# Attention with a soft mixture of experts: 64-row halves on TensorE, norms applied per row after a turn back, no detour through DRAM, and a new order

## The chip, the cores and the metric

The kernel runs on one core of one Trainium2 chip. The metric is device time in microseconds (us) of one execution. The kernel before took 525.68, 535.65 and 528.47 us in three runs, the median is 528.47 us. The core's engines are TensorE (PE; its weight loads are shown apart as PEld), VectorE (DVE), ScalarE (ACT), GpSimd (POOL) and SyncE (SP), whose queue issues nearly all transfers.

## The reference, cut to what matters

```python
# q, k, v: (8, 8, 576, 64); M_prev: (8, 8, 64, 64); z_prev: (8, 8, 64)
scores = np.where(causal, -1e9, q @ k.T / 8)
a = exp(scores - rowmax); a /= a.sum(-1) + 1e-9
local = a @ v
q_p = where(q > 0, q, exp(q) - 1) + 1
mem_out = (q_p @ M_prev) / (q_p @ z_prev + 1e-6)
attn = g * mem_out + (1 - g) * local          # g = sigmoid(beta), one per head
x = attn as (4608, 512)                       # row = batch and position, column = head and d
logits = x @ phi                              # 32 slots: 8 experts with 4 slots each
slot_input = softmax_over_rows(logits).T @ x
slot_out[e] = relu(slot_input[e] @ w1[e]) @ w2[e]     # 8 experts, 512 -> 1024 -> 512
out = softmax_over_slots(logits) @ slot_out
```

## The kernel before, in words

All data are fp32. The attention runs over 32 pairs n (8 batches with 4 pairs of heads; a pair's two heads lie on the row halves 0 to 63 and 64 to 127). For each pair the scores of 576 queries are cut into row blocks: three blocks of 128 queries for each head (q1, q2, q3, with 256, 384 and 512 keys) and blocks a, b, z in which 64 queries of both heads lie below each other. The q blocks are computed as three fp32r products of high and low parts with 64 contracted rows (`op_s`, L433), the two heads side by side in the array; a, b and z are fp32 products on all 128 rows (L427), with a q that was laid out block-diagonally in DRAM. DVE adds the mask and takes the row maximum (`op_max`, L462), ACT takes exponentials and row sums (`op_exp`, L470). TensorE then turns the probabilities in blocks of 128 by 128 (`op_t`, L560), ACT or DVE copy the turned blocks to SBUF (`op_te`), and `op_av` (L598) multiplies by v with an output whose rows are head and d and whose columns are queries. The output so has queries along its free axis, and the softmax sums and memory norms, which were found per row, have to be spread along the columns: they are turned (`op_rt`, L481), written to DRAM (`op_rrw`, `op_nrw`) and read back broadcast over 64 partitions (`op_rrr` into `rm`, L497; `op_nrr` into `rb`, L546). The factor `rb` is multiplied into phi(q) (`op_qn`, L550), the memory product adds to the output (`op_mema`, L592 and L593), and `op_mo`, `op_xe` (L626 to L637) multiply by `rm`, add, and leave the result in `xt`, which has d along partitions.

Every 512 rows of x form a group (9 groups) for the mixture: logits (`op_x1`, L646), running softmax, a turn of x (`op_x3`, L712), weighted sums of rows (`op_x4`, L725). The last group is done in the `y` steps after the last pair. Then come the experts (`f1`, `f1t`, `f2`) and the combination with its output transfers (`comb`).

The order is written out by hand as a list, `SEQ`: every step is emitted in that order, and `pin` makes each engine keep it; the digit behind a colon names the PSUM slot. `EV` says which engine makes a copy. PSUM has two score tiles of two banks (psS), three one-bank tiles (psT) and one output bank (psO). Expert weights are 64 tiles of 512 KB; `WORD` says where the first 44 of them go: 28 have a place of their own and can be loaded early, 16 go into tiles that the attention has freed. The other 20 are loaded in the expert stage, into places whose weights were used, and the output is staged in such places too.

Of the kernel before, what the change touches and what calls it, by code (L numbers as in the profile page):

```python
# [23 lines left out]
GROUPS = [
    [("q3h0", 0, 512), ("q3h1", 512, 512)],
    [("q2h0", 0, 384), ("b", 384, 128), ("q2h1", 512, 384), ("a", 896, 64)],  # L30
    [("q1h0", 0, 256), ("z", 256, 576), ("q1h1", 768, 256)],
]
# [11 lines left out]
}  # L44

SEQ = """
gate@0 loadq@1 loadm@0 loadk@1 loadm@1 loadv@0 qhi@0 qmin@0 kn@0 s.zb@0:0 qlo@0 qexp@0 s.b@0 s.a@0 kl@0 qmin@1 qphi@0
s.q3@0:1 max.b@0 max.a@0 exp.b@0 norm@0:0 max.q3h1@0 s.q2@0 neps@0 max.q3h0@0 exp.q3h1@0 nmk@0 max.q2h1@0 s.q1@0:1
exp.q3h0@0 max.zb@0 max.q2h0@0 s.z@0 kn@1 exp.q2h1@0 nred@0 kl@1 exp.q2h0@0 qhi@1 s.a@1:0 nrw@0 s.b@1 max.q1h0@0
s.zb@1 exp.a@0 loadq@2 t.1@0:1 max.a@1 qexp@1 max.zb@1 qlo@1 max.q1h1@0 t.2@0:2 max.z@0 exp.q1h0@0 nrr@0 t.0@0:0  # L50
te.2@0 max.b@1 s.q2@1 qphi@1 exp.z@0 s.q3@1:1 loadk@2 max.q2h1@1 exp.q1h1@0 max.q2h0@1 te.0@0 norm@1:2 rec@0 s.q1@1:0
neps@1 te.1@0 exp.b@1 nmk@1 rt@0:0 t.4@0:2 rte@0 qhi@2 max.q3h1@1 t.3@0:1 rrw@0 te.4@0 t.5@0:0 max.q3h0@1 exp.q2h1@1
s.z@1 te.3@0 exp.a@1 te.5@0 qn@0 s.a@2:1 s.zb@2 exp.q3h1@1 av.0@0 nred@1 rrr@0 max.z@1 av.2@0 kn@2 exp.z@1 loadk@3
av.1@0 loadq@3 max.a@2 kl@2 exp.q2h0@1 av.6@0 nrw@1 av.3@0 max.q1h0@1 exp.q3h0@1 memb@0:2 max.q1h1@1 s.b@2 loadv@1
mema@0:1 exp.q1h0@1 t.2@1:0 mo@0 qmin@2 loadm@2 s.z@2:0 nrr@1 te.2@1 xe.1@0 exp.q1h1@1 t.5@1:0 xe.0@0 qlo@2 t.1@1:1
rec@1 te.5@1 t.0@1:2 max.zb@2 max.b@2 qexp@2 rt@1:0 s.q2@2 rte@1 exp.a@2 qphi@2 rrw@1 te.1@1 s.q1@2 max.q2h1@2 te.0@1
t.4@1:0 max.q2h0@2 t.3@1:1 te.4@1 norm@2:2 te.3@1 neps@2 s.q3@2:1 rrr@1 exp.q2h0@2 nmk@2 max.q1h1@2 qhi@3 memb@1:0
kn@3 av.0@1 max.q1h0@2 loadq@4 qlo@3 exp.b@2 qn@1 exp.q1h0@2 av.3@1 max.z@2 av.6@1 exp.q2h1@2 kl@3 av.1@1 max.q3h0@2
exp.q1h1@2 av.2@1 nred@2 exp.q3h0@2 x3.0@0:1 nrw@2 exp.z@2 mema@1:2 mo@1 loadv@2 max.q3h1@2 loadk@4 s.q2@3:0 xe.1@1
nrr@2 exp.q3h1@2 s.q3@3:1 xe.0@1 x3e.0@0 rec@2 qmin@3 loadm@3 s.b@3 max.q3h1@3 t.4@2:2 qexp@3 max.q3h0@3 t.5@2:0  # L60
# [1030 lines left out]
```

## Time and profile before

| | |
|---|---|
| three runs | 525.68, 535.65, 528.47 us |
| span of the profiled execution | 529.8 us (no other time is given for it) |
| PE / PEld busy | 461.3 us / 307.6 us |
| DVE, ACT, POOL busy | 378.0, 331.8, 124.5 us |
| moved by DMA | 101.78 MB, mean 192 GB/s |

A busy time is the share in which at least one instruction of the engine was under way, with the time in which its result drains; the chain of work that ended last gives 34% to PE, 24% to DMA and 24% to DVE. On PE, two instructions stand in the trace for one fp32 product, and one for a turn or an fp32r product.

### The profile page before, as it was taken

To read this page: it belongs to the slowest core of one execution; us is meant where nothing else is said; L and a number is where in the kernel's file an instruction comes from. 1 tells how busy PE (TensorE), PEld (TensorE's weight loads), DVE (VectorE), ACT (ScalarE), POOL (GpSimd) and SP (SyncE) were. 2 spreads that over 40 slices of the span, in tenths; PEclk is the share of its full clock that TensorE was granted. 3 is DMA by queue.
4 is the path that set the end of the run, shared out by engine and by line. 5 is a ranking of instruction groups with operands and counts; after the bars stand their busy time and mean duration, and the time that the engine had idled before them with its cause. 6 is when DMAs were issued, how large, how long until landed. Compare 5 with 4: busy or idle time off the path is not lost.

```text
span 529.8 us, 12019 instructions
## 1 busy us (share of the span) xinstructions
PE 461.3 (87%) x4042; PEld 307.6 (58%) x4042; DVE 378.0 (71%) x1314; ACT 331.8 (63%) x969; POOL 124.5 (23%) x138
## 2 busy tenths in 40 slices
PE   8989899789998899999897987889988869799983
PEld 5656566556656566665665664656655546444541
DVE  7879788776788589789767877478887747334232
ACT  5777677666777577766786676566874837312232
POOL 4223122332213214235221332223314200000000
PEclk9999999989999999999999999799999979999997
DMA  6544654765466445554654674275564666899989
GB/s 200 181 142 133 186 178 132 217 203 162 137 172 181 138 128 171 140 155 134 196 153 145 187 202 123 58 176 152 157 188 142 214 191 178 304 415 410 382 297 323
DMA packets 66285, 101.78 MB, mean 192 GB/s; under 512 B 11248, under 2 KB 41520, under 8 KB 66224
## 3 DMA queue, kind: packets, MB, share of 16 engines
q1 hardware_dynamic: 65936, 100.93, 60.7%
q8 instruction: 32, 0.52, 0.4%
q14 instruction: 29, 0.24, 0.2%
q10 hardware_dynamic: 288, 0.09, 0.1%
HBM read 91.25 MB, written 9.73 MB: 191 GB/s over the span
## 4 chain that ended last, share of the span: by engine, by line
PE 34%; DMA 24%; DVE 24%; SPq 6%; ACT 4%; issue 4%; POOL 1%; DVEq 0%; POOLq 0%; ACTq 0%
DMA rm<-rs 9%; PE psT L560 6%; DVE q L462 5%; PE psS L427 5%; PE oa L598 4%; PE psS L433 4%; DVE zq L462 3%; DMA q<-in_M_dram 3%; DMA rs<-rts 3%; DMA k<-in_k_dram 3%; PE pf L947 3%; PE pf L930 2%; DVE at L358 2%; PE psT L592 2%; PE pp L990 2%
## 5 line engine op out<-in xcount | busy, mean ns | idle before, releaser
L355 ACT COPY at<-psT 128x256 f32<-128x256 f32 (+1 forms) x202 | 86.4, 479 | 53.5 <-PE psT L560 50.5
L470 ACT ACTIVATE q<-q,nm 128x512 f32<-128x512 f32 (+2 forms) x160 | 97.6, 613 | 17.2 <-DVE nm L462 17.0
L598 PE MATMUL oa<-at,mv 128*64 128x320 f32 (+4 forms) x640 | 94.0, 430 | 3.6 <-DVE at L358 1.4
L427 PE MATMUL psS<-k,qq 128*128 128x256 f32 (+2 forms) x320 | 67.7, 324 | 15.3 <-DVE nm L462 12.6
L462 DVE CUSTOM_DVE_ANT_0 q<-psS,mv 128x512 f32<-128x512 f32 (+1 forms) x128 | 76.1, 612 | 4.4 <-PE psS L433 2.5
L433 PE MATMUL psS<-K,X 64*128 64x512 f32 (+2 forms) x576 | 70.9, 367 | 8.6 <-DVE nm L462 6.8
L560 PE MATMUL psT<-cs,q 128*128 128x128 f32 x480 | 75.2, 280 | 3.3 <-DVE xt L633 1.4
L470 ACT ACTIVATE zq<-zq,nm 128x256 f32<-128x256 f32 (+2 forms) x128 | 67.7, 532 | 9.7 <-DVE nm L462 9.2
L427 PEld LDWEIGHTS psS<-k,qq 128*128 128x128 f32 x320 | 50.8, 195 | 27.2 <-DVE nm L462 18.2
L560 PEld LDWEIGHTS psT<-cs,q 128*128 128x128 f32 x480 | 57.3, 146 | 9.5 <-issue 3.2
L433 PEld LDWEIGHTS psS<-K,X 64*128 64x128 f32 x576 | 46.4, 189 | 27.0 <-issue 10.0
L598 PEld LDWEIGHTS oa<-at,mv 128*64 128x64 f32 x640 | 38.3, 138 | 39.0 <-issue 24.9
L560 PE MATMUL psT<-cs,zq 128*128 128x128 f32 x288 | 48.5, 283 | 2.8 <-DVE xt L633 1.0
L505 POOL TENSOR_SCALAR qp<-qq 128x576 f32<-128x576 f32 x19 | 31.4, 1650 | 68.2 <-PE psT L593 53.8
L626 DVE TENSOR_TENSOR xt<-oa,rm 128x448 f32<-128x448 f32 (+7 forms) x60 | 23.8, 436 | 30.3 <-DMA rm<-rs 25.4
L358 DVE COPY at<-psT 128x512 f32<-128x512 f32 (+1 forms) x59 | 32.4, 570 | 11.0 <-PE psT L560 9.7
L411 POOL TENSOR_TENSOR K<-k,K 128x512 fp32r<-128x512 f32 x25 | 32.4, 1295 | 33.3 <-ACT K L355 19.6
L550 DVE TENSOR_TENSOR qp<-qp,rb 128x576 f32<-128x576 f32 x32 | 27.6, 863 | 15.5 <-DMA rb<-rd 15.5
L560 PEld LDWEIGHTS psT<-cs,zq 128*128 128x128 f32 x288 | 34.9, 147 | 6.4 <-ACT at L355 1.7
L592 PE MATMUL psT<-qp,q 128*128 128x512 f32 x64 | 34.6, 622 | 2.9 <-DVE qp L550 1.9
L530 POOL TENSOR_TENSOR rn<-rn,rm 128x144 f32<-128x144 f32 x22 | 10.3, 467 | 100.2 <-ACT rn L523 57.4
L470 ACT ACTIVATION_READ_ACCUMULATOR q<-q,nm 128x1 f32 x160 | 31.1, 194 | 0.0
(207 smaller groups left out, 737.1 us busy)
## 6 DMA issues: line engine op xcount, KB each, us to landing
w<-in_w_dram SPq DMA_DIRECT2D x49, 512.0 KB
qq<-in_q_dram SPq DMA_DIRECT2D x32, 480.0 KB
mv<-in_v_dram SPq DMA_DIRECT2D x64, 160.0 KB
k<-in_k_dram SPq DMA_DIRECT2D x32, 288.0 KB
rb<-rd SPq DMA_DIRECT2D x64, 144.0 KB
rm<-rs SPq DMA_DIRECT2D x64, 144.0 KB
q<-in_M_dram SPq DMA_DIRECT2D x32, 80.0 KB
out_dram<-w SPq DMA_DIRECT2D x5, 512.0 KB
```

What stands on the lines that cost most here:

```text
L355: nc.scalar.copy(o, i)
L358: nc.vector.tensor_copy(out=o, in_=i)
L411: ALU_ENG[ev("kl", n)].tensor_tensor(out=K2[:, 1, :], in0=st[n]["k"][:, 0:512], in1=K2[:, 0, :].bitcast(F32), op=ALU.subtract)
L427: nc.tensor.matmul(ps[:, c + x0 - k0:c + x1 - k0], s["qd"][:, i], s["k"][:, x0:x1], start=True, stop=True)
L433: nc.tensor.matmul(ps[:, c0:c0 + N], X[ROW[h], x, 128 * i - 128:128 * i], K2[ROW[h], y, 0:N], start=(x, y) == (0, 0), stop=(x, y) == (0, 1))
L462: nc.vector.tensor_tensor_reduce(out=sm, in0=src, in1=msk, op0=ALU.add, op1=ALU.min, scale=-0.125, scalar=m0, accum_out=acc_o)
L470: nc.scalar.activation(sm, sm, AF.Exp, scale=-1.0, bias=s["nm"][:, J:J + 1], accum_out=s["sum"][:, J:J + 1])
L505: ALU_ENG[ev("qmin", n)].tensor_scalar(out=st[n]["qp"], in0=st[n]["q"], scalar1=0.0, scalar2=None, op0=ALU.min)
L550: ALU_ENG[ev("qn", n)].tensor_tensor(out=s["qp"], in0=s["qp"], in1=s["rb"], op=ALU.mult)
L560: nc.tensor.transpose(out=ps[:, 128 * x:128 * x + 128], in_=src[:, k0:k0 + 128], identity=ident)
L592: nc.tensor.matmul(om, s["m"][:, 0:128], s["qp"][:, 64:576], start=True, stop=True)
L598: nc.tensor.matmul(o[ROW[h], col:col + nx], vt[:, c, ROW[h]], at[:, a0 + hs * h:a0 + hs * h + nx], start=start, stop=stop)
```

## The change

The list of heads, pairs and groups stays, nearly every step of the attention is written anew.

- **Row halves.** For each pair and head, queries 64 to 575 form four blocks i of 128 with 192, 320, 448 and 576 keys. All are fp32r products of high and low parts on row halves (`s_part`); the fp32 products a, b, z are gone. The second head's keys are stored in reverse, so that its masked ends meet the first head's. Queries 0 to 63 of two pairs are handled together in 16 small side steps (`op_as` to `op_aad`).
- **Half turns.** A block of 128 by 128 is turned by two products, one for rows 0 to 63 and one for rows 64 to 127 (`turn`, with 64 columns of the identity moving), into two banks.
- **Product with v.** It works on 32-column quarters (`quarters`, `op_av`).
- **Turn back.** The output is copied (`op_oe`) and turned back so that queries lie on partitions (`op_u`, turns and memory products in one tile). Sums and norms are then one number per row: `op_dn` and `op_mu` apply them on DVE, POOL adds the two parts (`op_ad`). All writes to and reads from DRAM for norms are gone, and with them `op_rrw`, `op_rrr`, `op_nrw`, `op_nrr`, `op_qn`, `op_mo` and `op_xe`.
- **PSUM.** Scores, turns and `op_u` share three tiles of two banks (psD); psO and psM have one bank.
- **Loads.** One transfer brings q and k of a pair (`qk`, 544 KB), one v and M (`vm`, 544.5 KB), both into two tiles; a third (`au`, 385 KB) serves two pairs. They come 32, 32 and 16 times.
- **Weights.** `WORD` has 36 entries (18 with a place of their own, 18 in freed tiles); 28 are loaded in the expert stage.
- **Order.** `SEQ` and `EV` are new; the mixture's group of queries 0 to 63 (`AG`) comes before groups 6 and 7, and group 7 is the last.

```diff
-    def op_rrw(n):
-        rts = st[n]["rts"]
-        rd = st[n]["rs"] = drm.tile([2, S], F32, name="rs")
...
-    def op_nrw(n):
-        rd = st[n]["rd"] = drm.tile([4, 2, 144], F32, name="rd")
-        nc.sync.dma_start(out=rd.rearrange("g h (u x) -> (g h u) x", x=9), in_=st[n]["rq"])
...
-    def op_mema(n):
...
+    def s_part(n, ps, i, c, k0, k1):
+        s = st[n]
+        for x, y in ((0, 0), (1, 0), (0, 1)):
+            for h in range(2):
+                o = h * (S - LEN[i])
+                nc.tensor.matmul(ps[:, h, c:c + k1 - k0], s["X"][ROW[h], x, 128 * i:128 * i + 128], s["K"][ROW[h], y, o + k0:o + k1],
+                                 start=(x, y) == (0, 0), stop=(x, y) == (0, 1))
...
+    def turn(o, i, r):
+        nc.tensor.transpose(out=o, in_=i, identity=ident[ROW[r], ROW[r]])
+
+    def op_t(n, t):
+        s = st[n]
+        ps = s["t", t] = bank()
+        full = {"A": [(3, kb, h) for kb in range(4) for h in range(2)],
+                "B": [(2, kb, h) for kb in range(3) for h in range(2)],
+                "C": [(1, kb, h) for kb in range(2) for h in range(2)] + [(0, 0, h) for h in range(2)]}[t]
+        for x, (i, kb, h) in enumerate(full):
+            for r in range(2):
+                turn(ps[:, r, 64 * x:64 * x + 64], s["p", i][ROW[r], h, (128 * kb, 64 + 128 * (i - kb))[h]:][:, 0:128], r)
+        for x, i in {"A": (), "B": ((6, 3), (7, 2)), "C": ((6, 1), (7, 0))}[t]:
+            turn(ps[:, 1, 64 * x:64 * x + 64], s["p", i][ROW[1]].rearrange("a h x -> a (h x)")[:, LEN[i] - 64:LEN[i] + 64], 1)
...
+    def quarters(o, w, rhs, start, stop):
+        for j in range(4):
+            nc.tensor.matmul(o[32 * j:32 * j + 32], w[:, 32 * j:32 * j + 32], rhs[j // 2], start=start, stop=stop)
...
+        for kb in range(i + 1):
+            quarters(o, s["v"][:, kb], [at[:, 2 * kb + h, i].rearrange("a r x -> a (r x)") for h in range(2)], kb == 0, False)
+        quarters(o[:, 64:128], s["vb"][:, i], [atq[:, 3 - i]] * 2, False, True)
...
+    def op_u(n, u):
+        s, u = st[n], int(u)
+        ps = s["u", u] = bank()
+        for x in range(2):
+            i = 2 * u + x
+            for h in range(2):
+                turn(ps[:, h, 130 + 65 * x:194 + 65 * x], s["os"][ROW[h], 128 * i:128 * i + 128], h)
+        for x in range(2):
+            i = 2 * u + x
+            for h in range(2):
+                nc.tensor.matmul(ps[:, h, 65 * x:65 * x + 65], s["f"][ROW[h], 128 * i:128 * i + 128], s["m"][ROW[h]], start=True, stop=True)
...
+        nc.vector.tensor_tensor(out=w, in0=s["u", u][:, :, 0:260].rearrange("a h (x d) -> a h x d", d=65)[:, :, :, 0:64],
+                                in1=s["R"][:, u].rearrange("a h (x o) -> a h x o", o=1).broadcast_to([128, 2, 4, 64]), op=ALU.mult)
...
+        ALU_ENG[ev(f"ad.{u}", n)].tensor_tensor(out=o, in0=w[:, :, 0:2], in1=w[:, :, 2:4], op=ALU.add)
```

How the order on PE changes is seen in the steady middle. In the kernel before, around pairs 10 and 11, the rows of PE are these (a row is a line, the tile written and read, the output's partitions by columns, and how many products; 32 partitions are quarters, 64 are column halves, L433 works on row halves):

```order
L433 MATMUL psS_2030<-K_104,X 128x256 x6
L725 MATMUL psT_2063<-xk,ext 32x256 x4
L518 MATMUL psT_2070<-qp,q_1995 32x144 x4
L598 MATMUL oa<-at,mv 64x512 x2
L598 MATMUL oa<-at,mv 64x64 x2
L598 MATMUL oa<-at,mv 64x320 x2
L598 MATMUL oa<-at,mv 64x192 x2
L598 MATMUL psT_2102<-at,mv 64x64 x2
L598 MATMUL oa<-at,mv 64x448 x2
L433 MATMUL psS_2110<-K_104,X 128x512 x6
L592 MATMUL psT_2126<-qp,q_1822 128x512
L593 MATMUL psT_2102<-qp,q_1822 128x64
```

In the changed kernel, at about the same place (L391 scores, L426 half turns, L488 and L543 products on row halves, L454 quarters):

```order
L426 MATMUL psD_3557<-cs,p_3459 128x64 x14
L391 MATMUL psD_3576<-K,X 128x288 x6
L391 MATMUL psD_3589<-K,X 128x448 x6
L543 MATMUL psD_3604<-au 128x64 x4
L426 MATMUL psD_3611<-cs,os 128x64 x4
L488 MATMUL psD_3611<-vm,f 128x65 x4
L454 MATMUL oa<-at,vm 32x128 x4
L454 MATMUL oa<-at,vm 32x64 x4
L454 MATMUL oa<-at,vm 32x128 x8
L454 MATMUL oa<-at,vm 32x64 x4
L426 MATMUL psD_3654<-cs,x 128x64 x8
L426 MATMUL psD_3666<-cs,p_3515 128x64 x16
```

Before, the array changes its tile shape after one to six rows (row halves, quarters, column halves, full); now all but the quarters work on row halves, and the shape changes at `op_av` alone. Over the whole program the shape changes 275 times before and 143 times now.

The queue of SP before, for about one pair (`rd`, `rs` are the tiles in DRAM, `rb` and `rm` what is read back):

```order
L540 DMA rd<-rq 128x9
L391 DMA mv<-in_v_dram 64x640 x2
L546 DMA rb<-rd 64x4x144 x2
L396 DMA q_1995<-in_M_dram 128x160
L491 DMA rs<-rts 3x128 x2
L492 DMA rs<-rts 2x2x64
L493 DMA rs<-rts 2x1x64
L381 DMA qq<-in_q_dram 128x960
L749 DMA w_2077<-in_w_dram 128x1024
L386 DMA k<-in_k_dram 128x576
L497 DMA rm<-rs 64x576 x2
```

And now, for about two:

```order
L347 DMA qk<-in_qk_dram 128x1088
L354 DMA vm<-in_vm_dram 128x1089
L739 DMA w_2941<-in_w_dram 128x1024
L347 DMA qk<-in_qk_dram 128x1088
L522 DMA au<-in_au_dram 128x770
L354 DMA vm<-in_vm_dram 128x1089
```

Nothing that an engine has just computed goes through this queue any more, and an input load stands behind no such transfer.

## Rows read from the trace of the kernel before

**Rows 1.** The page, busy time of each engine over the span.
```profile
PE 461.3 (87%) x4042; PEld 307.6 (58%) x4042; DVE 378.0 (71%) x1314; ACT 331.8 (63%) x969; POOL 124.5 (23%) x138
```

**Rows 2.** Stretches: attention, joint, experts (us; busy and count; clock; DMA share; GB/s).
```profile
7.50:455.70 448.20, 396.86 (x3330) 273.68 (x3330) 347.14 (x1236) 310.02 (x923) 122.34 (x130) 0.98 0.55 162
455.70:469.70 14.00, 10.49 (x154) 7.63 (x152) 8.44 (x31) 4.32 (x14) 0.00 (x0) 1.00 0.99 397
469.70:529.90 60.20, 47.91 (x552) 23.36 (x552) 18.62 (x37) 14.53 (x28) 0.00 (x0) 0.94 0.96 360
```

**Rows 3.** Chain of work that ended last, its longest pieces in the attention (start, us, what).
```profile
309.95 5.84 DMA rm<-rs
...
423.79 8.10 DMA q<-in_M_dram
```

**Rows 4.** Waits of PE in the attention (us in total, times, longest us).
```profile
PE psS L427 <- DVE nm L462: 12.6, 18, 2.1
PE psT L518 <- DMA q<-in_M_dram: 10.2, 3, 5.0
```

**Rows 5.** Timeline of PE (start us, us, engine, line): full weights, 32 moving columns.
```profile
467.77 1.06 PE L862 MATMUL psT<-lt,xk 128*128 128x32 f32 x8
468.66 0.36 PE L877 MATMUL psT<-den,cs 128*128 128x1 f32 x2
```

**Rows 6.** Timeline of PE: row halves, quarters, row halves.
```profile
7.50 0.97 PE L433 MATMUL psS<-K,X 64*128 64x512 f32 x6
8.40 0.45 PE L518 MATMUL psT<-qp,q 128*32 128x144 f32 x8
8.79 0.80 PE L433 MATMUL psS<-K,X 64*128 64x384 f32 x6
```

**Rows 7.** Stretches cut between pairs of row halves, 384 columns, then 512.
```profile
63.39:63.57 0.18, 0.18 (x4) 0.18 (x4) 0.00 (x0) 0.18 (x1) 0.00 (x0) 1.00 0.62 128
63.97:64.20 0.23, 0.23 (x4) 0.19 (x2) 0.00 (x0) 0.23 (x1) 0.00 (x0) 1.00 0.96 381
```

**Rows 8.** Timeline of PE: column halves of 64 columns, then row halves.
```profile
62.79 0.28 PE L598 MATMUL psT<-at,mv 128*64 128x64 f32 x4
62.90 0.29 PE L598 MATMUL oa<-at,mv 128*64 128x64 f32 x4
63.12 1.49 PE L433 MATMUL psS<-K,X 64*128 64x384 f32 x12
```

**Rows 9.** Timeline of PE: 32 quarter products of 128 columns, then full ones.
```profile
124.01 1.08 PE L646 MATMUL psT<-xt,rm 128*32 128x128 f32 x32
125.07 0.43 PE L427 MATMUL psS<-k,qq 128*128 128x64 f32 x2
```

**Rows 10.** Timeline of PE: four full turns, then the next instruction.
```profile
211.80 0.60 PE L560 MATMUL psT<-cs,zq 128*128 128x128 f32 x4
212.24 0.56 PE L427 MATMUL psS<-k,qq 128*128 128x64 f32 x4
```

**Rows 11.** Groups on DVE by line (count, busy us, mean ns, idle before, releaser).
```profile
L550 DVE TENSOR_TENSOR qp<-qp,rb 128x576 f32<-128x576 f32 x32 | 27.6, 863 | 15.5 <-DMA rb<-rd 15.5
L626 DVE TENSOR_TENSOR xt<-oa,rm 128x448 f32<-128x448 f32 (+7 forms) x60 | 23.8, 436 | 30.3 <-DMA rm<-rs 25.4 <-PE oa L598 3.2 <-PE psT L593 1.2
L637 DVE TENSOR_TENSOR xt<-xt,psT 128x448 f32<-128x448 f32 (+7 forms) x60 | 23.4, 429 | 0.8 <-PE psT L592 0.7
```

**Rows 12.** Timeline of DVE: row maxima of 256, then of 512 columns.
```profile
199.90 0.42 DVE L462 CUSTOM_DVE_ANT_0 zq<-psS,mv 128x256 f32<-128x256 f32 x1
200.24 0.75 DVE L462 CUSTOM_DVE_ANT_0 zq<-psS,mv,nm 128x512 f32<-128x512 f32 x1
```

**Rows 13.** Group on ACT: exponentials of 576 keys.
```profile
L470 ACT ACTIVATE zq<-zq,nm 128x576 f32<-128x576 f32 x32 | 24.7, 772 | 4.4 <-DVE nm L462 4.4
```

**Rows 14.** Two stretches: PE waiting in the attention; the experts' loads.
```profile
330.00:340.00 10.00, 7.01 (x45) 6.10 (x46) 2.33 (x12) 2.67 (x7) 2.51 (x3) 0.66 0.26 71
470.00:500.00 30.00, 29.02 (x338) 13.04 (x332) 7.57 (x20) 5.57 (x12) 0.00 (x0) 1.00 1.01 405
```

More of the change, by code (lines that the diff above doesn't have):

```diff
@@ L227 @@
[L227 to L231 removed]
+QK = 512 + S
@@ L354, in act, with misc @@
+    def misc():
+        return psM.tile([128, 512], F32, name="psM")
     def act(o, i):
@@ new lines, in op_as, with op_amx @@
+    def op_as(n):
+        s = us[n]
+        ps = s["ps"] = bank()
+        for x in range(2):
+            for h in range(2):
+                nc.tensor.matmul(ps[:, h, 0:64], s["q"][ROW[h], x], s["k"][ROW[h], x], start=x == 0, stop=x == 1)
+    def op_amx(n, h):
+        s, h = us[n], int(h)
+        if "nm" not in s:
+            s["nm"] = sml.tile([128, 2], F32, name="anm")
+            s["p"] = spl.tile([128, 2, 64], F32, name="ap")
+        nc.vector.tensor_tensor_reduce(out=s["p"][:, h], in0=s["ps"][:, h, 0:64], in1=mask2, op0=ALU.add, op1=ALU.min,
+                                       scale=-0.125, scalar=3.0e38, accum_out=s["nm"][:, h:h + 1])
@@ new lines, in op_aav, with op_aoe, op_au @@
+    def op_aav(n):
+        s = us[n]
+        s["oa"] = misc()
+        for x in range(2):
+            quarters(s["oa"][:, 64 * x:64 * x + 64], s["v"][:, x], [s["at"][:, x]] * 2, True, True)
+    def op_aoe(n):
+        s = us[n]
+        s["os"] = spl.tile([128, 128], F32, name="aos")
+        ENG[ev("aoe", n)](s["os"], s["oa"][:, 0:128])
+    def op_au(n):
+        s = us[n]
+        ps = s["u"] = bank()
+        for h in range(2):
+            turn(ps[:, h, 65:129], s["os"][ROW[h]], h)
+        for x in range(2):
+            for h in range(2):
+                nc.tensor.matmul(ps[:, h, 0:65], pha[ROW[h], x], s["m"][ROW[h], x], start=x == 0, stop=x == 1)
@@ new lines, in op_x3, with op_x3e @@
+    def op_x3(g, c):
+        d, c = xs[g], int(c)
+        ps = d["p3", c] = bank()
+        for j in range(4):
+            for r in range(2):
+                turn(ps[:, r, 64 * j:64 * j + 64], d["x"][ROW[r], j, 128 * c:128 * c + 128], r)
+    def op_x3e(g, c):
+        d, c = xs[g], int(c)
+        d["xd", c] = dbl.tile([128, 4, 2, 64], F32, name="xd", bufs=4)
+        ENG[ev(f"x3e.{c}", g)](d["xd", c].rearrange("a j r x -> a r j x"), d["p3", c][:, :, 0:256].rearrange("a r (j x) -> a r j x", j=4))
@@ new lines, in op_x1, with op_x1l @@
+    def op_x1(g, c=None):
+        if c is None:
+            for c in range(4):
+                op_x1(g, c)
+            return
+        d, c = xs[g], int(c)
+        if c == 0:
+            d["p1"] = misc()
+        for j in range(4):
+            nc.tensor.matmul(d["p1"][32 * j:32 * j + 32, 0:128], ph[:, c, :], d["xd", c][:, j].rearrange("a r x -> a (r x)"), start=c == 0, stop=c == 3)
+    def op_x1l(g):
+        lt = xs[g]["lt"] = sml.tile([128, 128], F32, name="lt", bufs=1)
+        ENG[ev("x1l", g)](lt, xs[g]["p1"][:, 0:128])
```

1254 lines of the change are left out of this document (583 added, 671 removed), and 6 rows, old and new, of the table BANKS.

## The prediction, made before the changed kernel ran

> **What bounds the kernel now.** I read the busy times first. PE leads with 461.3 of 529.8 us, DVE and ACT are well below it [rows 1]. A share over the whole span mixes stages, so I cut it into stretches next: 7.5 us until the first scores, 448.2 us of attention, a joint of 14 us, 60.2 us of experts [rows 2]. The attention decides. In it PE is busy for 396.9 us and idle for 51; DVE has 347, ACT 310, POOL 122 [rows 2]. The experts are another matter: their loads and outputs move 360 GB/s with the DMA engines busy for 0.96 of the time [rows 2], so they are bound by bytes.
>
> Then the chain that ended last: its longest pieces in the attention are transfers of 6 to 8 us, the read back of `rm` and the late load of M [rows 3]. The waits of PE name DVE maxima (12.6 us) and M (10.2 us) [rows 4], and DVE itself waits 25.4 us for `rm` and 15.5 us for `rb` [rows 11]. So PE is the bound with about 11% of holes, and a large part of the holes leads back to transfers.
>
> **PE's work for one pair, before.** A busy PE includes draining, so I price by distances between starts. Row-half pairs run side by side: a pair of 512 columns takes 0.23 us, one of 384 takes 0.175 [rows 7]; by the line through both, 448 take 0.20, 320 0.15, 288 0.13, 256 0.12 (estimates). A full turn takes 0.11 us [rows 10]. A product whose weights have 128 columns never takes less than 0.111 us, however few columns move: eight took 0.89 us with 32 [rows 5]. Four quarters of 128 columns together take 0.11 us a pass (32 took 1.06 us with the change of shape) [rows 9], which is 0.86 ns a column; an fp32 product takes two passes.
>
> Scores 3 x (0.23 + 0.175 + 0.12) = 1.58. Blocks a, b, z: 512 columns x 2 x 0.86 ns = 0.88, and three small ones of 2 x 0.11: together 1.54. Norm and turn of the sums 0.36. 24 turns 2.64. Memory 576 x 2 x 0.86 ns + 0.11 = 1.10. Product with v 1600 x 2 x 0.86 ns = 2.75. Mixture, spread over the pairs, 1.05. Sum 11.0 us.
>
> To this comes the change of tile shape. From column halves to row halves, two pairs and the first new pair take 0.49 us from 62.90 to 63.39 where 0.11 + 0.175 would do: 0.20 lost [rows 7, 8]. Quarters to row halves lose 0.14 before the first start (8.40 to 8.79 for two passes of 0.12) and another 0.11 in the first pair, row halves to quarters 0.10 (8.79 and 7.50 against their neighbours) [rows 6]; quarters to full 0.18 [rows 9]. I take 0.17 on average. About 260 of the 275 changes lie in the attention, 8.1 a pair: 1.4 us. Sum 12.4 us a pair, 397 us for 32. That is the busy time of the row [rows 2], so the prices hold, and the 51 us of holes come on top.
>
> **The same for the change.** Scores 3 x (0.13 + 0.13 + 0.20 + 0.15 + 0.11) = 2.2 (192 columns at the floor of 0.11). Turns: 20 pairs and 4 single halves of p, 4 pairs of the output. The price of a pair of half turns isn't in the trace. Its moving part is short (64 columns x 0.86 ns = 0.06), but each half loads 128 columns of weights. Bounds: 0.06 if the load is hidden, 0.22 if the halves' loads follow one another. I take the floor of 0.11 [rows 5], since row halves do run side by side [rows 7]: 28 x 0.11 = 3.1, more than the 2.64 before, since the output's turns are new. Memory products: 4 pairs x 2 passes x 0.11 = 0.9. Product with v (1280 + 256) x 2 x 0.86 ns = 2.65. Side steps for queries 0 to 63: ten passes of 0.11 and 0.23 of quarters for two pairs, 0.7 a pair. Mixture 1.05. Sum 10.6 us. Half turns so save nothing; the gain in products is 0.4 us a pair, from a, b, z and the norms.
>
> The changes of shape fall to 143, some 130 of them in the attention, 4.1 a pair, at about 0.19 (to quarters 0.10 to 0.15, back 0.25) [rows 6]: 0.8 us. Sum 11.4 us a pair, 365 us for 32: **32 us less**, 19 of them from the shapes.
>
> **DVE, ACT, POOL.** Row maxima cover as many columns as before; one of 256 takes 0.34 us from start to start [rows 12]. DVE loses L550, L626 and L637 (74.8 us) [rows 11] and about 50 us of small groups, and gets 64 multiplications of 512 columns (about 0.65 each, as L637 by columns, 42 us), some 30 us of small row operations, 20 of side steps and 25 of copies: about 8 less. ACT has 10 fewer. Both stay below PE (340 and 300 us) and cost nothing while their work is on time. POOL goes from 122 to some 210 us (all high and low parts, `op_ad`, phi). It works two or three pairs ahead on double tiles; without that cover a pair's scores would wait nearly 4 us.
>
> **Holes.** The transfers for norms vanish, and each load goes out two or three pairs ahead. Left are PE's waits for softmax. The scores 3b and the turn A have between them scores 2, `u.1` and `av.0`, `av.1`: 0.6 + 0.67 + 0.9 + 0.4 of shape = 2.55 us. The chain beside it is a maximum (0.44), two exponentials of 576 keys (0.77 each) [rows 12, 13] and three handovers of about 0.2: 2.6 us, if both engines are free. Scores 10 and turn C have 2.6 us of PE work between them and a chain of about 3.0. Turn B reuses the tile of turn A, whose copies have 0.7 us of PE work to hide behind and need 1.0. That makes 0.1 to 0.5, 0.4 and 0.3: I take 1.4 us a pair, **45 us** (before: 51). Bounds: 14 us, if only such waits as PE now has for DVE remain [rows 4], and 78 us, below.
>
> **The rest.** Start 8 us (one more us for the masks behind 1.1 MB of loads). Joint 12 us: the last group's x is turned piece by piece earlier. Experts: 28 instead of 20 weights are loaded there, 8 x 0.52 MB = 4.2 MB more at 405 GB/s [rows 14] = 10 us, of which I take off 3 because the kernel before still had late loads in flight there: 67 us.
>
> Sum of the span: 8 + 365 + 45 + 12 + 67 = 497 us, against 529.8. The runs' median is 1.3 us below the span, so I predict **496 us**. In short: time = 451 + holes.
>
> **Rivals.**
> *Too few PSUM tiles* (the slow side). Scores, turns and `u` share three double banks, nine uses a pair; before, five tiles served them. If each use costs PE 0.3 us of waiting for the drain, holes are 9 x 0.3 x 32 = 86 us: 537. Against it: DVE and ACT would be only 75% to 80% busy. It makes the kernel no faster from 78 us of holes (0.27 a use), slower by 2% from 88. Chance 0.16, half of it within 2%.
> *No holes but the few of rows 4*: 14 us, 465. For it: the chain's long pieces are all transfers [rows 3]; against it: the tight turns. Chance 0.12.
> *The halves don't load side by side*: 24 pairs x 0.11 more x 32 = 84 us, 580. Against it: row-half pairs of 384 columns at 0.175 leave no room for two loads in a row [rows 7]. Chance 0.04.
> *The clock.* [...] Chance 0.04.
> *Issue.* About 8,600 products and as many weight loads stand against 4,042 each [rows 1]. If an instruction cost more than its array work, quarters would pay. Thirty-two took 1.06 us, 33 ns apiece with their loads [rows 9], so this needs 8,600 x 0.033 = 284 us at that rate, less than the 365. [...] Chance 0.02: 560.
>
> **How the numbers follow.** The forecast has 0.62; its own range, with holes of 30 to 65 us, is 481 to 516. With the rival of few holes below and half of the PSUM rival above, the range that holds 8 in 10 is 470 to 528. A difference of 2% (518 to 539) is about what a measurement of this kernel can tell. Faster: 0.62 + 0.12 = 0.74. Within: 0.08. Slower: 0.08 + 0.04 + 0.04 + 0.02 = 0.18.
>
> **What would show it.** Half turns at 0.11 us a pair; PE busy about 365 us in an attention of some 410; turns A and C waiting for ACT's exponentials; no transfer on the chain there; an expert stage of 65 to 69 us at 360 to 410 GB/s. I am wrong if a pair of half turns takes 0.2, if DVE or ACT passes 90% busy, if PE waits for tiles at most uses, or if a load again stands on the chain.

## The result, and the profile after

The changed kernel takes 507.6 us (median of four runs, 501.7 to 509.5) against 529.9 us for the kernel before in the same comparison; the ratio is 0.955 with a 95% interval of 0.945 to 0.965. It is faster by some 22 us. The forecast was 496 us with a range of 470 to 528. The profiled execution took 509.5 us, its span is 507.6. Two of the four runs, the profiled one among them, are over 1.5% above the fastest and don't count in the ratio; this trace, and that of the repeat below (e1, 515.9 us), so show 6 and 10 us more than the faster runs of the same kernel take.

The page of the kernel after, busy time of each engine, the granted clock over the span, and the queue that brings instructions (packets, MB, share of 16 engines):

```profile
PE 417.1 (82%) x8597; PEld 340.9 (67%) x8597; DVE 368.9 (73%) x1315; ACT 318.1 (63%) x972; POOL 207.1 (41%) x259
...
PEclk8999899989898989999898999997999997599995
...
q8 instruction: 68, 1.11, 0.9%
```

The same queue on the page of the kernel before:

```profile
q8 instruction: 32, 0.52, 0.4%
```

PE fell from 461.3 to 417.1 us [rows 1], but its share of the span fell too: it works less and waits more. The three stretches of the kernel after, cut as [rows 2] (us; busy and count of PE, PEld, DVE, ACT, POOL; clock; DMA share; GB/s):

```profile
7.85:422.90 415.05, 353.21 (x7968) 309.96 (x7968) 344.33 (x1258) 299.44 (x934) 203.86 (x251) 0.95 0.43 145
422.90:436.93 14.03, 8.51 (x55) 6.00 (x56) 4.20 (x18) 2.20 (x8) 0.72 (x1) 0.57 0.11 38
436.93:507.60 70.67, 50.77 (x568) 23.17 (x568) 17.12 (x30) 13.84 (x26) 0.00 (x0) 0.89 0.93 343
```

The attention is 33 us shorter than in [rows 2], with PE busy for 353 us and idle for 62. So the forecast of 365 + 45 was too high for the work and too low for the holes. The experts take 70.7 us, 10 more than before, at 343 GB/s.

No transfer of data stands among the long pieces of the attention's chain any more, unlike [rows 3]. What ends PE's idle time there, first in the list of [rows 4], then for the weight loads, which come ahead of the products (us in total, times, longest):

```profile
PE oa L454 <- issue: 6.9, 5, 3.0
PE psD L426 <- DVE nm L415: 6.2, 10, 1.5
PE psD L426 <- ACT at L306: 6.1, 13, 1.3
```
```profile
PEld oa L454 <- issue: 16.0, 37, 3.2
PEld psD L391 <- issue: 8.5, 8, 2.6
```

The list of the loads in the kernel before:

```profile
PEld oa L598 <- issue: 24.9, 96, 0.6
```

"issue" means that the engine waited for nothing that the profile shows. In [rows 4] a maximum of DVE led the list; here a few long stops without a reason do. (The loads had such gaps before too, but many short ones; new is their length.) The longest in the timeline of weight loads (start, us, what, and in brackets the idle time before it):

```profile
102.42 0.55 PEld L454 LDWEIGHTS oa<-at,vm 128*32 128x32 f32 x14
106.13 0.37 PEld L454 LDWEIGHTS oa<-at,vm 128*32 128x32 f32 x14 [3.17 <-issue]
```

It falls into the middle of one group of quarters, whose operands had long been there. So I numbered the instructions of PE's queue in the trace (products, weight loads, semaphore instructions): there are 17,397, and the page counts 68 packets (1.11 MB, so 16 KB each) on the instruction queue, room for 68 times 256. Nine times in the attention PE stops for more than 0.45 us ahead of an instruction that waits for no semaphore, 13.6 us in all, and each time that instruction's number is 193 modulo 256. Each of these stops ends 1.3 to 1.6 us after a packet of the instruction queue has landed. So these are late instructions: a packet of 256 instructions lasts 6.7 us here on average (420 us for 16,158; the expectations below say 6.2, a slip), and 16.5 us in the kernel before, which has no such stop. The packet for the next 256 mostly starts less than 2 us after the one ahead of it began to be executed; ahead of the nine stops it starts 3 to 6 us after. In those moments loads were in flight; the stretch before the longest stop (DMA share and GB/s at the end, against 0.43 and 145 over the attention):

```profile
97.80:103.70 5.90, 5.22 (x131) 4.55 (x128) 5.36 (x20) 4.34 (x16) 5.07 (x7) 1.00 0.73 256
```

Two more readings. A pair of half turns: twelve of them start within 0.37 us, until the next group of two (timeline of products):

```profile
201.86 0.54 PE L426 MATMUL psD<-cs,p 64*128 64x64 f32 x12
202.20 0.38 PE L391 MATMUL psD<-K,X 64*128 64x288 f32 x1
202.23 0.28 PE L426 MATMUL psD<-cs,p 64*128 64x64 f32 x2
```

That is 0.062 us a pair, where the forecast took 0.11. And the copies of the turn tiles wait for each other (what ended the idle time of ACT and of DVE):

```profile
ACT at L306 <- DVE at L309: 29.9, 51, 2.0
```
```profile
DVE at L309 <- ACT at L306: 19.8, 33, 1.8
```

### The profile page after: what moved, and what is told of

It is laid out like the page before. It is cut to its first block, busy times and chain, and to the rows that moved or that the text cites. A ratio compares the mean times of both kernels' runs of the same rounds, so it can differ in the third digit from the quotient of the medians.

```text
span 507.6 us, 20499 instructions
## 1 busy us (share of the span) xinstructions
PE 417.1 (82%) x8597; PEld 340.9 (67%) x8597; DVE 368.9 (73%) x1315; ACT 318.1 (63%) x972; POOL 207.1 (41%) x259
## 3 DMA queue, kind: packets, MB, share of 16 engines
q8 instruction: 68, 1.11, 0.9%
## 4 chain that ended last, share of the span: by engine, by line
DVE 34%; PE 30%; ACT 18%; DMA 8%; issue 5%; POOL 1%; SPq 0%; POOLq 0%; DVEq 0%; ACTq 0%
DVE p L415 11%; ACT p L423 8%; PE oa L454 8%; PE psD L426 7%; PE psD L391 7%; DVE at L309 6%; ACT at L306 5%; DVE w L500 4%; DMA w<-in_w_dram 3%; PE psD L488 2%; DVE f L382 2%; DMA x<-in_w_dram 2%; DMA xa<-in_w_dram 2%; ACT xd L306 1%; DVE R L495 1%
## 5 line engine op out<-in xcount | busy, mean ns | idle before, releaser
L423 ACT ACTIVATE p<-p,nm 128x192 f32<-128x192 f32 (+3 forms) x256 | 155.3, 609 | 22.0 <-DVE nm L415 21.6
L391 PE MATMUL psD<-K,X 64*128 64x288 f32 (+3 forms) x960 | 104.3, 339 | 22.2 <-DVE anm L550 4.0
L454 PE MATMUL oa<-at,vm 128*32 128x128 f32 (+1 forms) x3584 | 105.5, 268 | 9.5 <-issue 6.9
L415 DVE CUSTOM_DVE_ANT_0 p<-psD,mk 128x192 f32<-128x192 f32 (+3 forms) x256 | 110.2, 476 | 4.0 <-PE psD L391 3.3
L454 PEld LDWEIGHTS oa<-at,vm 128*32 128x32 f32 x3584 | 94.2, 114 | 22.4 <-issue 16.0
L306 ACT COPY at<-psD 128x512 f32<-128x512 f32 (+3 forms) x162 | 68.1, 451 | 53.3 <-DVE at L309 29.9
L391 PEld LDWEIGHTS psD<-K,X 64*128 64x128 f32 x960 | 78.9, 197 | 31.5 <-issue 8.5
L513 POOL TENSOR_TENSOR x<-w 128x256 f32<-128x256 f32 x64 | 49.6, 774 | 103.1 <-DVE w L500 77.8
L426 PE MATMUL psD<-cs,p 64*128 64x64 f32 x1408 | 65.2, 228 | 12.9 <-DVE nm L415 2.9
L426 PEld LDWEIGHTS psD<-cs,p 64*128 64x128 f32 x1408 | 57.8, 143 | 18.4 <-issue 4.3
L500 DVE TENSOR_TENSOR w<-psD,R 128x512 f32<-128x512 f32 x64 | 44.3, 692 | 4.8
L488 PE MATMUL psD<-vm,f 64*128 64x65 f32 x512 | 43.9, 282 | 1.2 <-issue 1.2
L488 PEld LDWEIGHTS psD<-vm,f 64*128 64x128 f32 x512 | 38.7, 199 | 1.4 <-issue 1.4
L426 PE MATMUL psD<-cs,os 64*128 64x64 f32 x256 | 23.5, 242 | 5.1 <-ACT at L306 1.5
## 6 DMA issues: line engine op xcount, KB each, us to landing
vm<-in_vm_dram SPq DMA_DIRECT2D x32, 544.5 KB, 3.6
```

Of the source, the lines that this page charges most:

```text
L306: nc.scalar.copy(o, i)
L391: nc.tensor.matmul(ps[:, h, c:c + k1 - k0], s["X"][ROW[h], x, 128 * i:128 * i + 128], s["K"][ROW[h], y, o + k0:o + k1], start=(x, y) == (0 ...
L415: nc.vector.tensor_tensor_reduce(out=s["p", i][:, h, k0:k1], in0=s["s", u][:, h, c:c + k1 - k0], in1=maskq[:, o + k0:o + k1], op0=ALU.add, ...
L423: nc.scalar.activation(p, p, AF.Exp, scale=-1.0, bias=s["nm"][:, 2 * i + h:2 * i + h + 1], accum_out=s["sum"][:, i // 2, h, i % 2:i % 2 + 1])
L426: nc.tensor.transpose(out=o, in_=i, identity=ident[ROW[r], ROW[r]])
L454: nc.tensor.matmul(o[32 * j:32 * j + 32], w[:, 32 * j:32 * j + 32], rhs[j // 2], start=start, stop=stop)
```

## The experiments

The runs e1 to e4, e5 to e8, e9 to e11 and e12 were made on four chips. For all runs I read one stretch, from the first scores to the turn of the mixture's running maximum, just ahead of the experts; called the attention from here on. "Work" is PE's busy time less half of what lay in spells at the low level of the clock (0.50, where the trace shows 1.00 otherwise), that is, an estimate of its busy time at the full clock. "Clock" is that other half. "Late" is the sum of the stops at instruction 193 modulo 256. All in us; the median and the ratio are of the whole kernel.

| run | median | ratio to before (95%) | attention | work | clock | idle | of it late |
|---|---|---|---|---|---|---|---|
| before | 529.9 | 1 | 456.6 | 394.4 | 8.4 | 53.8 | 0 |
| after | 507.6 | 0.955 (0.945 to 0.965) | 419.9 | 334.1 | 20.4 | 65.3 | 13.6 |
| e1, after again | 506.7 | 0.961 (0.950 to 0.971) | 425.5 | 333.3 | 24.2 | 68.0 | 16.3 |
| e2, column halves | 498.5 | 0.947 (0.940 to 0.954) | 410.7 | 337.9 | 16.6 | 56.2 | 0 |
| e3, copies by bank | 504.7 | 0.960 (0.950 to 0.971) | 419.2 | 333.4 | 24.8 | 61.1 | 10.6 |
| e4, e2 and e3 | 498.2 | 0.947 (0.937 to 0.957) | 409.7 | 337.0 | 18.0 | 54.8 | 0 |
| e5, full turns | 519.1 | 0.980 (0.973 to 0.987) | 427.5 | 378.1 | 5.1 | 44.3 | 3.1 |
| e6, loads behind | 506.1 (one run) | | 407.1 | 334.6 | 12.3 | 60.2 | 4.0 |
| e7, shapes | 514.1 | 0.969 (0.964 to 0.974) | 423.9 | 351.5 | 18.8 | 53.6 | 3.6 |
| e8, control of e7 | 499.9 | 0.937 (0.927 to 0.948) | 410.6 | 338.6 | 12.7 | 59.4 | 3.0 |
| e9, copies apart | 499.0 | 0.948 (0.942 to 0.954) | 409.6 | 336.7 | 18.0 | 55.0 | 0 |
| e10, fillers | 500.4 | 0.954 (0.944 to 0.964) | 412.8 | 371.0 | 1.7 | 40.2 | 0 |
| e11, before without detour | 483.7 | 0.918 (0.911 to 0.924) | 406.9 | 391.3 | 0 | 15.5 | 0 |
| e12, one engine a tile | 490.0 | 0.930 (0.923 to 0.938) | 402.2 | 341.6 | 11.5 | 49.1 | 0 |

The stretch in the kernel before and in the changed one:

```profile
7.50:464.14 456.64, 402.83 (x3418) 277.76 (x3418) 352.11 (x1253) 312.67 (x932) 122.34 (x130) 0.98 0.56 166
```
```profile
7.84:427.69 419.85, 354.56 (x7984) 310.70 (x7985) 345.96 (x1264) 300.03 (x935) 204.58 (x252) 0.95 0.43 144
```

**The yardstick.** The changed kernel once more.

> The changed kernel once more, as the yardstick for the other runs of this row (its trace before: 415 us of attention with PE busy for 353 and idle for 62). All theories: about 505 us. The theory of late instructions says that PE's unexplained stops (no semaphore waited for, over 0.45 us) stand again at every instruction whose number is 193 modulo 256, and that they add up to some 13 us again, if the loads fall the same way.

506.7 us, and seven stops at 193 modulo 256, six of them at the very instructions of the first trace (3777, 6337, 6593, 7873, 11969, 16065); in e3, with the same products, there are seven again. Over all traces of this study there are 38 such stops. The only other gaps of that length without a semaphore (0.5 to 1.0 us, beside products of 448 or 512 columns that last as long, in part at the low clock) are not counted.

**Fewer instructions for the same work.** The product with v on column halves.

```diff
-        for j in range(4):
-            nc.tensor.matmul(o[32 * j:32 * j + 32], w[:, 32 * j:32 * j + 32], rhs[j // 2], start=start, stop=stop)
+        for j in range(2):
+            nc.tensor.matmul(o[ROW[j]], w[:, ROW[j]], rhs[j], start=start, stop=stop)
```

> The product with v is written as two 128x64 column halves, one for each head, instead of four 128x32 quarters: the same sums, the same columns moved, 56 products fewer a pair (and as many weight loads), so about 12,300 instead of 15,900 products and loads in the attention. Theory of late instructions (256 of PE's instructions come in one transfer of 16 KB, and where that transfer queues behind loads, PE stops until it is there): a page then lasts 8 us instead of 6.2, the nine stops of 13 us vanish nearly all and one or two low spells of the clock with them: attention 398 to 405 us, time 490 to 497. Theory of the drains (PE's holes are waits for softmax and copies alone): nothing changes but by chance, attention 412 to 418. Third: half weights of 64 columns load more slowly than quarters; then a pass of 128 columns takes over 0.12 us instead of 0.109 and PE's busy time grows by 5 us or more.

498.5 us (496.4 to 499.6) beside 506.7 (502.3 to 515.9) for the changed kernel on the same chip. The instruction queue and the attention of this run:

```profile
q8 instruction: 53, 0.87, 0.7%
```
```profile
7.89:418.61 410.72, 354.50 (x6064) 309.98 (x6065) 346.85 (x1264) 300.12 (x935) 204.34 (x252) 0.96 0.44 147
```

All late stops are gone, with 1,920 products fewer; a packet lasts 8.5 us. PE's work stayed within 4 us (337.9 beside 334.1), less than the 5 us or more that a slower load of half weights was to cost. The gain, 8 us by the medians and 9 us of attention between the traces, is less than the 13.6 us of stops: the other waits grew by 4.5 us. The attention of 410.7 us lies between the two ranges (398 to 405, 412 to 418), so the time fits neither theory. That the stops vanish, here and in the four later runs whose packets last 8.2 us or more (e4, e9, e10, e12), is what the theory of late instructions said and the theory of the drains alone doesn't explain.

**Loads out of the way.** The same instructions, other traffic.

```diff
     def op_w(x):
+        if x < 18 and x not in late:
+            late.append(x)
+            return
...
+    for x in list(late):
+        op_w(x)
```

> The first 18 loads of expert weights (9.4 MB) are moved out of the attention, behind it; the rest stays. The experts then last some 23 us longer, so only the attention counts (yardstick: 409 to 415 us). Theory of late instructions, with the loads as the cause of the delay: of the stops at instruction 193 modulo 256, those that fell on three loads with one of w (instructions 3777, 7873, 8641) or on w with au (6337) shrink from 1.3 to 5.0 us to under 1 us or vanish; those that fell on vm and qk alone (6593, 11969) stay at 0.5 to 3 us. Attention shorter by 5 to 10 us. Rival, that the stops have nothing to do with the loads (each page is late by the same process in PE): all stops stay as they were.

The stops at 3777, 6337, 7873 and 8641, which had fallen on a load of w, are under 0.45 us; 6593, on vm and qk alone, stays with 0.72 us (before 2.11). 11969 was to stay and went; 10689 and 14529 are new, with 0.65 and 1.27 us, and 15553 and 16065 stay, with 0.78 and 0.59. In all 4.0 us instead of 13.6, and the attention:

```profile
7.88:415.01 407.13, 346.93 (x7984) 303.98 (x7985) 346.15 (x1264) 299.85 (x935) 204.95 (x252) 0.97 0.39 127
```

This run alone doesn't show the loads as the cause. On the same chip e5, e7 and e8 have 3.0 to 3.6 us of stops with all loads in place, and e3 lacks the stops at 3777 and 8641 with them in place too. The packets themselves say more. In the seven traces with stops I set beside each of the attention's 438 packets what the loads moved in the 2 us after the packet ahead of it began to be executed. Beside 153 of them nearly nothing moved (DMA share under 0.05): 147 of these started within 2.5 us, and none brought a stop. Of 55 at a share of 0.9 or more, 32 started later than that; and all 38 stops have a share of 0.12 or more. So packets come late where loads are in flight. That fewer loads mean fewer stops isn't shown by itself, and how the two queues share the DMA engines wasn't tried.

**Half turns undone.** Full turns of p in the changed kernel.

```diff
-            for r in range(2):
-                turn(ps[:, r, 64 * x:64 * x + 64], s["p", i][ROW[r], h, (128 * kb, 64 + 128 * (i - kb))[h]:][:, 0:128], r)
+            nc.tensor.transpose(out=flatp(ps)[:, 128 * x:128 * x + 128], in_=s["p", i][:, h, (128 * kb, 64 + 128 * (i - kb))[h]:][:, 0:128], identity=ident)
```

> The changed kernel with one part undone: the 20 turns of p for a pair are full turns of 128x128 again (the four single halves, the turns of the output and all else stay). The full turns stand between row halves, so the changes of tile shape go from 143 to about 287. By the prediction's price (a pair of half turns at 0.11 us, like a full turn) the turns themselves cost the same, and only the shapes add 144 x 0.17 = 25 us, less some 8 us for late instructions, since 1,280 fewer products and loads are fetched: about 525. By the price that the trace of the changed kernel shows (0.062 us a pair), 20 x 0.048 x 32 = 31 us come on top: about 555. If shapes cost nothing where PE has holes anyway, 505 and 530.

519.1 us. (With full turns the copies read the tile in another order, too.) PE's work rose by 44.0 us: 31 for the turns at the measured price, so 13 for 144 changes of shape, 0.09 each. But the time rose by only 12 by the medians, and the attention by 7.6 between the traces:

```profile
8.10:435.58 427.48, 383.18 (x7345) 326.30 (x7345) 341.72 (x1264) 301.81 (x935) 204.79 (x252) 0.99 0.42 141
```

The clock is 0.99 instead of 0.95 (15 us less lost to it), the late stops fall by 10 us, and the rest of the idle time by 10. (The late stops are about as few in every run on this chip, so their part may not be the turns'.) That is where the gain of the half turns went: of 44 us of work saved, 36 came back between these two traces as holes, low clock and late instructions. None of the expected times is met. The nearest, 525, rests on the price of 0.11, which the trace contradicts; the work is what the other one has, with cheaper shapes, and the holes took most of it up.

**The price of a change of shape.** A dose of quarters between half turns, and as many half turns as its control.

```diff
+            if t == "B" and x in (1, 3):
+                extra(ps[:, 0, 384:512])
...
+    def extra(o):
+        nc.tensor.matmul(o[0:32, 0:32], cs[:, 0:32], cs[:, 128:160], start=True, stop=True)
```

> Two extra products of one 128x32 quarter with 32 columns (weights and data are constants, the result isn't used) stand in the midst of turn B of every pair, between half turns: 128 more changes of tile shape (143 to 271) and 64 extra products, 256 more products and loads in all. Theory that a change of shape costs 0.17 us each on PE's path: 128 x 0.17 = 22 us, and 64 x 0.06 = 4 us for the products: 530 to 533. If a change costs only the drain that the next product's wait hides, 510.

> The control of the run before: the same number of extra products at the same places, but as half turns of a constant on the rows 0 to 63, so that no shape changes. 128 half turns, one after another at about 0.06: 8 us of PE work at most, part of it in holes. All theories: 506 to 514. The difference between the two runs divided by 128 is the price of a change.

The attentions of the dose and of the control:

```profile
7.78:431.71 423.93, 370.32 (x8112) 320.30 (x8113) 341.47 (x1264) 301.14 (x935) 204.91 (x252) 0.95 0.43 143
```
```profile
7.81:418.42 410.61, 351.23 (x8113) 307.97 (x8113) 345.58 (x1264) 300.11 (x935) 204.58 (x252) 0.97 0.44 148
```

The work differs by 12.9 us and the medians by 14.2, over 128 changes: 0.10 to 0.11 us each, not 0.17. The dose lies between its two expectations (510 and 530), the control below its own (506 to 514); it was even faster than the changed kernel without it (ratios of 0.937 and 0.961 to the kernel before). Its trace has 3.0 us of late stops instead of 13.6 and 8 us less lost to the clock: the added products shift which instructions stand at the ends of the packets when loads are in flight. But e5, e6 and e7 on the same chip have about as few stops; whether it is the shift or the chip wasn't tested.

**The copies that wait for each other.** First by PSUM bank (e3, and e4 with the column halves), then with targets that don't interleave (e9).

```diff
+        if t != "C":
+            r, nb = int(x[1]), (8, 6)[t == "B"]
+            e(at[:, 0:nb, i, r], s["t", t][:, r, 0:64 * nb].rearrange("a (c x) -> a c x", x=64))
+            return
```

> The copies of turn tiles A and B are divided by PSUM bank (one copy takes bank 0, the other bank 1) instead of by key blocks, which read both banks each. Same columns, same engines. Now ACT waits 30 us for DVE's copies and DVE 20 us for ACT's, always of the same tile. Theory of the drains: those waits come from both copies reading the same bank; divided, the two run side by side, a tile is free 0.5 us earlier, twice a pair, and PE's holes shrink by 0.2 to 0.4 us a pair: 6 to 13 us, time 493 to 500. If the mutual waits stay, they come from the target or the tile as a whole. Theory of late instructions: at most 3 us, since a faster PE meets more late pages.

> Both edits of the two runs before this. If late instructions and drains are two separate causes, the gains add: 480 to 490 us. If one hides behind the other, the time is that of the better one alone.

> Column halves and copies by bank as in the run of both, and the target of the copies is laid out with the row half outermost, so that the two copies of a turn tile touch neither the same bank nor interleaved addresses. In the run of both ACT still waited 28 us for DVE's copies and DVE 19 us for ACT's. Theory that the program makes the second copy wait because the targets interleave: both waits fall under 10 us, the copies of tiles A and B run side by side, and the attention gets 3 to 10 us shorter than the 409.7 us of that run (time 488 to 495). If the waits stay, they come from elsewhere and the time stays at 498. If the waits go and the time stays, the copies weren't what PE waited for.

e3: 504.7 us, e4: 498.2, e9: 499.0, the last two like e2. ACT's wait for DVE's copies in e3 and in e9:

```profile
ACT at L306 <- DVE at L309: 29.6, 49, 2.0
```
```profile
ACT at L306 <- DVE at L309: 27.7, 49, 1.1
```

Both guesses fell. In e2, e3 and e9 alike the second copy starts within 0.06 us of the first one's end 84 times, while copies of different tiles overlap 24 or 25 times. (Counted are copies that follow one another. Taken tile by tile, ACT and DVE change 118 times within a turn tile in each of these traces, and never do their copies overlap.) So it is sharing one tile between two engines that makes the second wait, whatever bank or target. How that wait comes into the program wasn't read.

The last run therefore gives each tile to one engine.

```diff
+EV.update({f"te.{x}@{n}": "v" if x[0] == "B" else "a" for n in range(B * NP) for x in ("A0", "A1", "B0", "B1", "Bq", "C0", "C1", "Cq")})
```

> Column halves; the fillers and the moved zeroing in the joint alone (none in the attention); and every copy of a turn tile goes to one engine: tiles A and C to ACT, B to DVE (now three of four tiles are shared by both engines, and the second copy starts 0.03 us after the first has ended, 84 times in the trace, whatever bank or target the copies have). Theory of the drains: the mutual waits of ACT and DVE (28 and 18 us) vanish, both tiles drain side by side, the attention goes from 411 to 398 to 406 us. Rival: the cycle through DVE's maxima and ACT's exponentials bounds the attention, not the drains; then the waits go and the attention stays within 407 to 414 us. Joint by either 2 us shorter than 9.2 (last turn of the mixture's maximum to the experts' first product). Time 488 to 493, or 495 to 499.

It stands on the column halves and on e10's edits of the joint (below). 490.0 us, 17 less than the changed kernel and 7% less than the kernel before; only e11, which leaves the norms out, is faster. Its attention, joint and experts:

```profile
7.68:409.85 402.17, 353.10 (x6077) 306.23 (x6078) 333.73 (x1266) 299.40 (x933) 204.58 (x252) 0.97 0.45 150
409.85:416.72 6.87, 6.61 (x49) 4.46 (x50) 2.58 (x13) 1.73 (x7) 0.00 (x0) 1.00 0.01 2
416.72:484.80 68.08, 52.16 (x568) 25.73 (x568) 17.41 (x30) 13.86 (x26) 0.00 (x0) 0.84 0.96 355
```

The 84 waits are 0, the overlaps 44, and from the first to the last scores it takes 387.4 us, where e2 takes 395.4. So one engine a tile is worth 8 us between these traces, as the theory of the drains said, and this lies beside the late instructions, not in their place. (By the medians e12 is 8.5 us ahead of e2, 2.4 of them from the joint.) Not separated is that the run also moves work: DVE is busy for 13 us less than in e2 (333.7 and 346.9), ACT as long as there.

**Fillers.** Products of constants in PE's holes, on the column halves. The cut shows those of the attention; others stand in the joint, where the zeroing of the mixture's tile on POOL was moved too.

```diff
+        if t != "B":
+            for r in range(2):
+                nc.tensor.matmul(ps[:, r, 0:256], cs[ROW[r], 0:128], cs[ROW[r], 0:256], start=True, stop=True)
```

> Column halves, and filler products of constants whose results nobody uses: one pair of row halves of 256 columns ahead of turns A and C of every pair (0.25 us each, 16 us in all if nothing hides them), and nine full products of 256 columns (0.44 us each at the high clock) in the holes of the joint; the zeroing of the mixture tile moves behind the last sum on POOL. Theory of the clock (PE's low spells come from its holes and cost about half of the work in them): low spells in the attention fall from 36 us to under 20, which gives back 8 us, and the fillers hide in waits, so the attention stays at 405 to 413 us (410.7 without); the joint, at the low clock now, gets 2 to 4 us shorter. Rival (the clock hardly matters, PE is late anyway): attention 418 to 426 us, joint as long as before.

500.4 us. The attention and the joint:

```profile
8.05:420.86 412.81, 372.65 (x6333) 323.55 (x6334) 343.64 (x1264) 299.96 (x935) 204.41 (x252) 1.00 0.43 146
420.86:427.72 6.86, 6.61 (x49) 4.45 (x50) 2.57 (x13) 1.73 (x7) 0.00 (x0) 1.00 0.00 0
```

The joint without fillers, in e2:

```profile
418.61:427.85 9.24, 7.17 (x39) 5.27 (x40) 2.58 (x13) 1.61 (x7) 0.00 (x0) 0.50 0.00 0
```

The fillers cost twice what I had reckoned, 33 us of work beside e2. The attention grew by 2: 15 us came back from the clock, which no longer falls, and 16 were hidden in waits. The joint, from the turn of the maximum to the experts' first product, takes 6.9 us at clock 1.00; without fillers, in e2, it takes 9.2 at 0.50. POOL does nothing in either stretch, and DVE and ACT do as much, so the gain there is the clock's. So the low clock costs time, as the theory of the clock said, but in the attention no more than fillers of this size cost.

**The detour alone.** The kernel before, with the transfers of the norms left out and ones in their place (its output isn't normalised, so its time isn't that of a finished kernel).

```diff
     def op_rrr(n):
+        return
...
     def op_nrr(n):
+        st[n]["rb"] = rr
+        return
```

> The kernel before, without the detour of the norms through DRAM: the writes and reads of the row sums and norms are left out and both multiplications use a constant tile of ones (so the output isn't normalised; all products, turns and the multiplications themselves stay). Theory of the prediction (a large part of PE's 51 us of holes in the attention leads back to these transfers): attention 448 us now, 415 to 432 without, time 495 to 513. Rival (the holes are waits for softmax, the transfers were hidden): 440 to 448, time 520 to 530.

483.7 us. Page and attention:

```profile
PE 451.7 (94%) x4042; PEld 301.7 (63%) x4042; DVE 375.8 (78%) x1315; ACT 330.1 (69%) x969; POOL 124.5 (26%) x138
```
```profile
7.50:414.35 406.85, 391.33 (x3420) 271.45 (x3419) 350.25 (x1254) 311.08 (x932) 122.35 (x130) 1.00 0.44 141
```

The attention is 50 us shorter, more than either theory gave: 38 us of idle time, 8 of low clock, 3 of work. The old tiling with its full turns and quarters keeps PE busy for 96% of the attention once no transfer stands in its way. Whether PE waited for the norms themselves or for the loads that stood behind them in SP's queue isn't separated. Beside this run the attention of the changed kernel is 13 us longer, although PE has 57 us less work in it: 50 us more idle time and 20 of low clock outweigh them.

## Why the prediction was right, and where it wasn't

The direction is right and the time lies in the range, 12 us above the point. The sum came close because two terms were off in opposite directions: 365 of work and 45 of holes were forecast for the attention, 410 together, and by the cut of [rows 2] it has 415, with 334 of work, some 20 of low clock and 62 of holes. That these add up so nearly is luck.

- **What bounds the kernel before.** Right, and stronger than I put it: e11 shows that 38 of 54 us of PE's holes led back to the transfers of the norms, and the 8 us of low clock with them.
- **PE's work.** The sum was 365 us, the trace has 334 at the full clock. Row by row, per pair: turns 2.0 us (forecast 3.1), scores 2.7 (2.2), product with v 2.9 (2.65), memory products 1.0 (0.9), side steps 0.8 (0.7), mixture 1.0 (1.05); the excess of scores and products, 0.9, holds the changes of shape (0.8). The step that failed is "I take the floor of 0.11": 28 pairs of half turns at 0.062 are 1.3 us less than that for each pair of heads, in the rows 1.1. The lower bound, 0.06, was the truth. A floor read from fp32 products with 128 weight columns [rows 5] doesn't hold for turns of row halves, nor for every fp32 product: in the trace of before, of 163 with 64 columns that another such product follows, 63 are followed within 0.06 us.
- **Changes of shape.** Their number was right; their price, 0.17 to 0.19, is 0.10 by e7 and e8 and 0.09 by e5. If that holds for the kernel before too, which no run tested, then 18 of the 397 us that seemed to prove the prices were something else.
- **DVE, ACT, POOL.** 344, 299 and 204 us against 340, 300 and 210 forecast.
- **Holes.** 62 us instead of 45, by the cut of [rows 2]. The waits that I named add up to 0.8 to 1.2 us a pair, 26 to 38 us in all; the 1.4 that I took was already above them. 13.6 of the 62 are late instructions, for which the sum had no term. I had weighed issue as a rival, but by what one instruction costs the array (33 ns), and so found that 8,600 of them fit; I never asked how 256 instructions get there while loads are in flight. That rival at 0.02 was the right place with the wrong price: no run shows a rate that would give its 560 us, and twelve half turns in 0.37 us are 31 ns each. The 0.2 us that the softmax chain had for a handover no run shows either; in the trace of before ACT starts 0.035 us after the end of the DVE instruction that it waited for, DVE 0.038 after PE's and PE 0.053 after ACT's (medians of 40, 91 and 18 waits).
- **The clock.** I had it as all or nothing at 0.04, on an estimate that no run shows. It came in a small dose: 44 of 420 us at the low level (0.50), which costs 20 us (8 before). It nearly goes away with fillers (e10: 2 us) or more work (e5: 5 us), and wholly where PE hardly waits (e11). Idle time alone doesn't set it: the kernel before and e7 have the same 54 us and lose 8 and 19.
- **Too few PSUM tiles.** The 86 us of this rival didn't come; the number of tiles wasn't varied. What showed is two engines draining one tile, 8 us (e12). My 0.3 us a pair for turn B waiting for the tile of turn A was of that size, 10 us, for another mechanism.
- **The formula "time = 451 + holes"** failed as a way of thinking. It takes PE's work as given and holes as added, but after the change PE isn't the bound alone: 44 us more work costs 8 us of attention (e5; 12 of time by the medians), 33 us more cost 2 (e10). The work that the half turns saved mostly became idle time. That DVE has as much to do as before (344 against 347 us in [rows 2]) fits this; shown is only the copies' part, 8 us.
- **The rest.** Start 7.85 (8). Joint 14.0 instead of 12, with PE at a clock of 0.57. Experts 70.7 instead of 67: the 4.2 MB cost the full 10 us, and the 3 that I took off weren't there.

So the change gains 37 us in the attention (33 by the cut of [rows 2]) because it takes away a detour that cost about 50, and pays some of that back. Beside e11 the new tiling's 57 us less of work became holes and low clock, and 13 us more besides; but e11 doesn't apply the norms, and it is this tiling that applies them without a detour. The experts take 10 of the 33 us back, which leaves 22.

## What to carry to other kernels

Before you price a change that doubles the number of TensorE's instructions, divide them into packets of 256 and compare the time that a packet lasts with the time that one takes to come when loads are in flight; here 16.5 us a packet was safe, 8.2 to 8.5 us too, and 6.4 to 7.4 us cost 3 to 16 us in all. Before you take saved work off the time one for one, try the old work without its waits: here the old tiling without the detour, though no finished kernel, was faster than the new one, and of the 44 us of work that half turns save only 8 to 12 were time. Let one engine drain a PSUM tile where the copies of its parts don't overlap anyway, as in e2, e3 and e9; here that was worth 8 us (e12).

## What the runs showed of the hardware that I hadn't expected

- PE stopped at the end of packets of 256 instructions, for up to 5.0 us (e1): 38 such stops in seven traces, all at the same place modulo 256.
- A pair of half turns (two 64-row halves) costs 0.062 us within a run of twelve, a full turn 0.11 [rows 10].
- A change of tile shape costs 0.10 us of PE's work by 128 of them (e7, e8), less than single rows suggest [rows 6, 8, 9].
- 33 us of useless products cost 2 us of attention (e10): 15 came back as they keep the clock at 1.00 instead of 0.96, and 16 lay in waits.
